# Two-stage attention on one core: every engine's order laid out by a plan inside the kernel, and stage 1 unfolded from an SBUF copy

## The chip, the cores and the metric

One core of a Trainium2 chip runs the whole kernel. The core has five engines with a queue each: TensorE (PE: matmuls, and PEld for the loading of its stationary operand), VectorE (DVE), ScalarE (ACT), GpSimd (POOL), and SyncE (SP), which here only issues DMAs. Each engine works off its own queue strictly in order; engines wait for each other by semaphores. The metric is the device time of one execution in microseconds (us), the median of several runs.

## The reference, cut to what matters

```python
# stage 1: attention in a window of 64, batch 8, 8 heads, 576 positions, head size 64
scores = q @ k.T / 8;  mask = (rel >= 0) & (rel < 64)
attn = softmax(where(mask, scores, -1e9))
x = (attn @ v).transpose(0, 2, 1, 3).reshape(8, 576, 512)
# stage 2: four experts e with causal attention of head size 64 over x, gated by the best two
logits = x @ w_gate;  w = softmax of the two largest logits, 0 for the others
q, k, v = x @ wq[e], x @ wk[e], x @ wv[e]
a = softmax(where(causal, q @ k.T / 8, -1e9))
out += w[e] * (a @ v @ wo[e])
```

All is float32. `wq` and `wk` are scaled by 8, so that the logits of stage 2 spread widely.

## The kernel before, in words

**Stage 1** works on blocks of 64 queries and two heads. Eight such blocks make a *unit* `u`, and there are 36 units; nine units make two batches. A unit has three steps:

- `s1_qk(u)`: 16 small matmuls into two PSUM banks `s1_u_0`, `s1_u_1` (tag `s`, five banks in all). ACT (L146) and DVE (L150) gather them into the SBUF tile `sm1_u`. Then comes the softmax: DVE takes the largest (L152), POOL subtracts (L153), ACT exponentiates (L154), DVE sums and inverts (L155 to L157), and POOL multiplies (L158).
- `s1_t(u)`: four transposes of `sm1_u` on PE into one PSUM bank `t1_u` (tag `t`, three banks in all; L168). The bank is unfolded into the SBUF tile `pt1_u`: for each half `e`, ACT copies 64 partitions (L172) and DVE multiplies the same 64 partitions by a mask (L173); afterwards POOL masks both ACT copies at once (L176).
- `s1_av(u)`: 16 small matmuls of `pt1_u` with V into the bank `o1_u` (tag `t`; L187), which ACT and DVE turn into `xh` and `xl`, a high and a low part (L200, L201).

**Stage 2** needs `xh`, `xl` of a whole batch. `s2_v`, `s2_k`, `s2_q` project (`v2ps`, `kps`, `qps`, tag `s`, L269 to L271); `s2_mm` makes the scores of two experts (banks `s2_…`, tag `s`, L385); `s2_soft` reads them on DVE (L400), exponentiates on ACT (L404) and weights on POOL (L441); `s2_t` transposes on PE (L450, banks `t2_…`, tag `t`) and ACT copies into `pt2` (L457 to L490); `s2_av_mm` multiplies by V (`o2`, tag `t`, L509); `s2_o` makes the output (`ops`, tag `s`, L530, and a DMA).

**What sets the order.** Each step has a position in time, worked out from tables of numbers (`POS`, `BPOS`, `LEAD`, `LAG`). The steps are sorted by position and called. One unit of position is half a batch of stage 2. Tile's own scheduler then decides what each queue holds: before position 1.0 and after 15.5 it orders all engines; between the two PE keeps the order of the calls (`manual_schedule` for PE), and the scheduler orders ACT, DVE and POOL.

Of the kernel before, what the change touches and what calls it, by code (L numbers as in the profile page):

```python
# [8 lines left out]
F32 = mybir.dt.float32  # L9
F32R = mybir.dt.float32r  # L10
# [7 lines left out]
NP = NH // 2  # L18
# [16 lines left out]

@with_exitstack
def window_attention_moe_attention(ctx: ExitStack, tc: tile.TileContext, qT, kT, vW,
                                   wg, wq, wk, wv, wo, out):
    nc = tc.nc
# [20 lines left out]

    P2 = [const.tile([128, 1024 * (part + 1)], F32, name=f"p2_{part}") for part in range(2)]
# [21 lines left out]
    make_identity(nc, ident)  # L83
# [45 lines left out]
    def s1_qk(u):  # L129

        banks = [psum.tile([128, 4, 128], F32, tag="s", bufs=5, name=f"s1_{u}_{x}") for x in range(2)]
        for x, j, p, b in tiles(u):
            c0 = 64 * int(b == 0)
            for h in range(2):
                r, o = slice(64 * h, 64 * h + 64), 64 * (h ^ x)
                nc.tensor.matmul(banks[x][o:o + 64, j, c0:], lhsT=pairs[p][0][r, 64 * b:64 * b + 64],  # L136
                                 rhs=pairs[p][1][r, 64 * b + c0:64 * b + 128], start=True, stop=True)
# [25 lines left out]
    def s1_t(u):  # L163

        ps = psum.tile([128, 4, 128], F32, tag="t", bufs=3, name=f"t1_{u}")
        sm = SM.pop(u).rearrange("r x j c -> r (x j c)")
        for i in range(4):
            nc.tensor.transpose(ps[:, i], sm[:, 128 * i:128 * i + 128], ident)  # L168
        t = PT1[u] = work.tile([128, 4, 2, 128], F32, tag="pt1", bufs=2, name=f"pt1_{u}")
        for e in range(2):  # L170
            r = slice(64 * e, 64 * e + 64)
            nc.scalar.activation(t[64:128, :, e], ps[r], AF.Copy)  # L172
            nc.vector.tensor_mul(t[0:64, :, e], ps[r],  # L173
                                 tri[r].rearrange("r a c -> r (a c)")[:, None, :].to_broadcast([64, 4, 128]))
        own_half = t[64:128].rearrange("r i e (a c) -> r (i e a) c", a=2)
        nc.gpsimd.affine_select(out=own_half, in_=own_half, pattern=[[0, 16], [1, 64]], base=0,  # L176
                                channel_multiplier=-1, compare_op=OP.is_ge, fill=0.0)
# [3 lines left out]
    def s1_av(u):  # L181
        t = PT1.pop(u)
        o = psum.tile([128, 8, 64], F32, tag="t", bufs=3, name=f"o1_{u}")
        for i, (x, j, p, b) in enumerate(tiles(u)):
            for h in range(2):
                c = 64 * (h ^ x)
                nc.tensor.matmul(o[64 * h:64 * h + 64, i], lhsT=pairs[p][2][:, h, b],  # L187
                                 rhs=t[:, 2 * x + j // 2, j % 2, c:c + 64], start=True, stop=True)
            if b == BLK - 1:
                freed.append(p)  # L190
# [82 lines left out]
    def s2_v(b, j):  # L273


        ps = psum.tile([128, 512], F32, tag="s", bufs=5, name=f"v2ps_{b}_{j}")
        for c in range(NP):
            if j < 4:
                xh, xl = (y[b][:, S * c + 128 * j:S * c + 128 * j + 128] for y in (XH, XL))
            else:  # L280
                xh, xl = (XT[b, x][:, c].rearrange("r a c -> r (a c)") for x in range(2))
            three(ps[:, :260], xh, xl, whi["v"][:, c], wlo["v"][:, c], c == 0, c == 3)
        src = ps[:, :256].rearrange("r (p s c) -> r p s c", p=2, s=2)
        dst = [V2[(b + i) % 2].rearrange("r j (p s) c -> r j p s c", s=2) for i in range(2)]
        if j < 4:
            nc.scalar.activation(dst[0][:, j, :, 0], src[:, :, 0], AF.Copy)
            vo = work.tile([128, 2, D], F32, tag="vo", bufs=2, name=f"vo_{b}_{j}")
            nc.scalar.activation(vo, src[:, :, 1], AF.Copy)
            for x in range(2):
                nc.gpsimd.tensor_scalar(dst[0][64 - 64 * x:128 - 64 * x, j, :, 1], vo[64 * x:64 * x + 64],  # L290
                                        1.0, 1.0, op0=OP.mult, op1=OP.mult)
        else:
            for i in range(2):
                for s in range(2):
                    nc.scalar.activation(dst[i][64 * s:64 * s + 64, 4, :, s], src[64 * i:64 * i + 64, :, s], AF.Copy)
        nc.vector.tensor_copy(L[b % 2][:, j], ps[:, 256:260])

    def s2_gate(b, j0, j1):
# [6 lines left out]
        tc.keep_in_program_order(nc.vector.tensor_tensor(g4[:, 0], lf, le, op=OP.is_gt))  # L305
# [27 lines left out]
    def proj(b, name, pr, half):  # L333
# [40 lines left out]
    def s2_mm(b, pr, k):  # L374
        banks = SB[b, pr, k] = [psum.tile([128, 512], F32, tag="s", bufs=5, name=f"s2_{b}_{pr}_{k}_{e}")
                                for e in range(2)]
        for i, key, n in SCORES[k]:
            q = slice(128 * i - 128, 128 * i)
            for x, (w, m) in enumerate(((0, 0), (0, 1), (1, 0))):
                for e in range(2):  # L380
                    r = slice(64 * e, 64 * e + 64)
                    rhs = KT[b, pr][r, m, key:key + n]
                    if e:
                        rhs = rhs.rearrange("r (a c) -> r a c", c=64)[:, ::-1]
                    nc.tensor.matmul(banks[e][:, at(i, e):at(i, e) + n], lhsT=QT[pr][r, w, q], rhs=rhs,  # L385
                                     start=x == 0, stop=x == 2)

# [55 lines left out]
    def s2_t(b, pr, part, k):  # L443
# [15 lines left out]
        if part == 0 and k == 0:  # L459
            for e in range(2):  # L460
                for i in (1, 2):
                    one(256 * e + 128 * i - 128, i, e, 0)
            nc.scalar.activation(pt[:, :, 64:320], ps.rearrange("r (e c) -> r e c", e=2), AF.Copy)
        elif part == 0 and k == 1:
            for e in range(2):
                one(128 * e, 2, e, 1)
            one(256, 1, 0, 1)
            one(384, 2, 0, 2)
# [6 lines left out]
        elif k < 2:  # L475
            for c in range(2):
                for i in (3, 4):
                    one(256 * c + 128 * i - 384, i, k, c)
            nc.scalar.activation(pt[:, k, 0:512], ps, AF.Copy)  # L479
        elif k == 2:  # L480
            for e in range(2):
                for i in (3, 4):
                    one(256 * e + 128 * i - 384, i, e, 2)
            nc.scalar.activation(pt[:, :, 512:768], ps.rearrange("r (e c) -> r e c", e=2), AF.Copy)
        else:
            for e in range(2):
                one(128 * e, 4, e, 3)
            one(256, 3, 0, 3)
            one(384, 4, 0, 4)
# [13 lines left out]
    def s2_av_mm(b, pr, part):  # L503
# [3 lines left out]
        for a, (c, x, w, q0) in enumerate(AVS[part]):  # L507
            for h in range(2):
                nc.tensor.matmul(o[64 * h:64 * h + 64, q0:q0 + w], lhsT=V2[b % 2][:, c, 2 * pr + h],  # L509
                                 rhs=PT2[part][:, h, x:x + w], start=a == 0, stop=a == len(AVS[part]) - 1,  # L510
                                 skip_group_check=True)

# [157 lines left out]
```

## Time and profile before

| | |
|---|---|
| median of 3 runs | 580.79 us (579.72 to 580.87) |
| profiled execution, its own time | 579.19 us |
| its span, from the first to the last instruction | 577.5 us |
| mean granted TensorE clock | 0.949 |
| PE busy / DVE / ACT / POOL | 482.2 / 358.8 / 321.9 / 230.5 us |
| instructions | 14663 |

The profiled execution took 1.7 us more than its span, and the median lies 1.6 us above the profiled execution. A window row gives, for a stretch of the span, its length, then the busy time of each engine with the number of instructions, and the granted clock. A row of the timeline gives start, duration, engine, line, operation and tiles (buffer numbers left out), and in brackets the idle time just before it with what ended it. A row of the waits gives who waited for whom: total, number of times, and the longest.

### The profile page before, as it was taken

To read this page: it belongs to the slowest core of one execution; us is meant where nothing else is said; L and a number is where in the kernel's file an instruction comes from. 1 tells how busy PE (TensorE), PEld (TensorE's weight loads), DVE (VectorE), ACT (ScalarE), POOL (GpSimd) and SP (SyncE) were. 2 spreads that over 40 slices of the span, in tenths; PEclk is the share of its full clock that TensorE was granted. 3 is DMA by queue.
4 is the path that set the end of the run, shared out by engine and by line. 5 is a ranking of instruction groups with operands and counts; after the bars stand their busy time and mean duration, and the time that the engine had idled before them with its cause. 6 is when DMAs were issued, how large, how long until landed. Compare 5 with 4: busy or idle time off the path is not lost. (4 is left out here: it accounts for less than half of the span.)

```text
span 577.5 us, 14663 instructions
## 1 busy us (share of the span) xinstructions
PE 482.2 (84%) x5672; PEld 430.0 (74%) x5672; DVE 358.8 (62%) x1178; ACT 321.9 (56%) x965; POOL 230.5 (40%) x403
## 2 busy tenths in 40 slices
PE   4488859599697987959789895996969889999996
PEld 3377758588586967858688794985858888899874
DVE  5977857558366774746656675574746567556452
ACT  3555455647357573655547565473555756565671
POOL 5656343532445342253333534244334442241330
PEclk9999978989799997979989899898989989999999
DMA  8574411122252222221333220231224100010112
GB/s 308 221 223 150 134 42 45 44 86 77 82 188 72 83 78 84 60 75 52 104 144 123 85 86 37 86 100 51 77 80 147 58 2 22 19 56 2 38 38 92
DMA packets 20630, 51.29 MB, mean 89 GB/s; under 512 B 2768, under 2 KB 3280, under 8 KB 20560
## 3 DMA queue, kind: packets, MB, share of 16 engines
q1 hardware_dynamic: 20560, 50.35, 26.4%
q8 instruction: 45, 0.74, 0.5%
q14 instruction: 25, 0.20, 0.1%
HBM read 40.90 MB, written 9.44 MB: 87 GB/s over the span
## 5 line engine op out<-in xcount | busy, mean ns | idle before, releaser
L404 ACT ACTIVATE p<-p,r 128x192 f32<-128x192 f32 (+3 forms) x128 | 77.3, 605 | 50.6 <-DVE r L424 29.5
L441 POOL TENSOR_SCALAR p<-p,r 128x192 f32<-128x192 f32 (+3 forms) x128 | 72.7, 586 | 65.8 <-DVE r L437 44.0
L173 DVE TENSOR_TENSOR pt<-t,tri 64x512 f32<-64x512 f32 x72 | 49.4, 687 | 38.5 <-ACT pt L172 36.8
L168 PE MATMUL t<-ident,sm 128*128 128x128 f32 x144 | 27.8, 325 | 48.8 <-POOL sm L158 48.6
L187 PE MATMUL o<-pt,v 128*64 128x64 f32 x1152 | 49.0, 250 | 22.1 <-POOL pt L176 22.1
L400 DVE CUSTOM_DVE_ANT_0 p<-s,causal 128x320 f32<-128x320 f32 (+3 forms) x160 | 66.5, 472 | 0.7
L187 PEld LDWEIGHTS o<-pt,v 128*64 128x64 f32 x1152 | 44.0, 162 | 29.6 <-POOL pt L176 25.3
L172 ACT ACTIVATE pt<-t 64x512 f32<-64x512 f32 x72 | 42.5, 591 | 39.6 <-PE t L168 26.8
L450 PE MATMUL t<-ident,p 128*128 128x128 f32 x384 | 52.5, 276 | 11.7 <-ACT pt L479 11.4
L176 POOL TENSOR_SCALAR_AFFINE_SELECT pt<-pt 64x1024 f32<-64x1024 f32 x36 | 41.6, 1155 | 51.2 <-ACT pt L172 21.4
L154 ACT ACTIVATE sm<-sm 128x512 f32<-128x512 f32 x36 | 22.7, 631 | 67.1 <-POOL sm L153 67.1
L155 DVE TENSOR_REDUCE st<-sm 128x8 f32<-128x512 f32 x36 | 24.7, 685 | 56.5 <-ACT sm L154 56.4
L168 PEld LDWEIGHTS t<-ident,sm 128*128 128x128 f32 x144 | 18.9, 164 | 54.4 <-POOL sm L158 53.5
L158 POOL TENSOR_TENSOR sm<-sm,st 128x512 f32<-128x512 f32 x36 | 38.3, 1065 | 52.8 <-DVE st L157 32.2
L153 POOL TENSOR_TENSOR sm<-sm,st 128x512 f32<-128x512 f32 x36 | 38.5, 1070 | 49.3 <-DVE st L152 39.8
L450 PEld LDWEIGHTS t<-ident,p 128*128 128x128 f32 x384 | 42.9, 141 | 17.0 <-ACT pt L479 13.5
L509 PE MATMUL o<-pt,v 128*64 128x128 f32 (+3 forms) x896 | 55.4, 280 | 0.0
L136 PE MATMUL s<-k,q 64*64 64x128 f32 (+1 forms) x1152 | 49.1, 301 | 6.3 <-DMA k<-in_kT_dram 6.3
L509 PEld LDWEIGHTS o<-pt,v 128*64 128x64 f32 x896 | 51.0, 152 | 1.6 <-ACT pt L457 0.4
L136 PEld LDWEIGHTS s<-k,q 64*64 64x64 f32 x1152 | 38.1, 152 | 14.9 <-DMA q<-in_qT_dram 7.0
L385 PE MATMUL s<-kt,qt 64*128 64x256 f32 (+2 forms) x480 | 45.1, 323 | 0.3 <-DVE qt L359 0.2
L269 PE MATMUL kps<-xh,wkhi 128*128 128x320 f32 (+1 forms) x128 | 41.5, 324 | 0.0
(127 smaller groups left out, 1263.6 us busy)
## 6 DMA issues: line engine op xcount, KB each, us to landing
v<-in_vW_dram SPq DMA_DIRECT2D x32, 576.0 KB, 4.0
k<-in_kT_dram SPq DMA_DIRECT2D x32, 320.0 KB, 4.0
q<-in_qT_dram SPq DMA_DIRECT2D x32, 288.0 KB, 3.1
out_dram<-out SPq DMA_DIRECT2D x32, 256.0 KB, 2.0
out_dram<-out SPq DMA_DIRECT2D x8, 128.0 KB, 2.3
pt<-in_wv_dram SPq DMA_DIRECT2D x1, 512.0 KB, 8.8
pt<-in_wk_dram SPq DMA_DIRECT2D x1, 512.0 KB, 7.9
pt<-in_wq_dram SPq DMA_DIRECT2D x1, 512.0 KB, 8.7
```

The source lines that it names most:

```text
L136: nc.tensor.matmul(banks[x][o:o + 64, j, c0:], lhsT=pairs[p][0][r, 64 * b:64 * b + 64], rhs=pairs[p][1][r, 64 * b + c0:64 * b + 128], star ...
L168: nc.tensor.transpose(ps[:, i], sm[:, 128 * i:128 * i + 128], ident)
L172: nc.scalar.activation(t[64:128, :, e], ps[r], AF.Copy)
L173: nc.vector.tensor_mul(t[0:64, :, e], ps[r], tri[r].rearrange("r a c -> r (a c)")[:, None, :].to_broadcast([64, 4, 128]))
L176: nc.gpsimd.affine_select(out=own_half, in_=own_half, pattern=[[0, 16], [1, 64]], base=0, channel_multiplier=-1, compare_op=OP.is_ge, fill ...
L187: nc.tensor.matmul(o[64 * h:64 * h + 64, i], lhsT=pairs[p][2][:, h, b], rhs=t[:, 2 * x + j // 2, j % 2, c:c + 64], start=True, stop=True)
L385: nc.tensor.matmul(banks[e][:, at(i, e):at(i, e) + n], lhsT=QT[pr][r, w, q], rhs=rhs, start=x == 0, stop=x == 2)
L400: nc.vector.tensor_tensor_reduce(out=dst, in0=ps, in1=mask, scale=1.0, scalar=3.0e38, op0=OP.add, op1=OP.min, accum_out=to)
L404: nc.scalar.activation(p, p, AF.Exp, bias=r2[:, 0, x:x + 1], scale=-1.0, accum_out=r2[:, 1, x:x + 1])
L441: nc.gpsimd.tensor_scalar(p, p, r2[:, 3, x:x + 1], 1.0, op0=OP.mult, op1=OP.mult)
L450: nc.tensor.transpose(ps[:, col:col + 128], P2S[pr][part][:, at:at + 128], ident)
L509: nc.tensor.matmul(o[64 * h:64 * h + 64, q0:q0 + w], lhsT=V2[b % 2][:, c, 2 * pr + h], rhs=PT2[part][:, h, x:x + w], start=a == 0, stop=a ...
```

## The change

Three things are changed. No position in the tables is.

1. Calls to the engines are recorded by a class `Plan` and not issued at once. A call becomes an entry with its engine, its tiles, its position (`at`) and a length in ns from formulas for each engine. Matmuls inside `nc.block()` are one entry that isn't broken up.
2. `Plan.link` finds which entries must follow which, from the regions that they read and write. `Plan.order` then walks through time with a clock for each engine: whenever an engine is free, it takes, of the entries whose inputs are done by the lengths and whose buffers are free, the one with the earliest position. The entries are issued in the order in which they were taken, and `manual_schedule` for all engines keeps that order.
3. `s1_t` copies the whole bank `t1_u` to an SBUF tile `ft_u` with one ACT instruction. DVE multiplies from `ft_u`, and POOL masks from `ft_u` into `pt1_u`, one half each, so that there are two POOL instructions of half the size.

Since all instructions come out of one loop, every instruction carries the line of that loop in the changed program (L227).

```diff
+class Plan:
+    OVERLAP = {"V": 85, "A": 105, "G": 30, "P": 0, "S": 0}
+    SWITCH = 105
+    HOP = 40
...
+    def length(self, engine, name, outs, ins):
+        n = outs[0].free_size()
+        psum = any(x.space == PSUM for x in ins)
+        if engine == "A":
+            return (165 if psum else 205) + 0.83 * n + (230 if len(outs) > 1 else 0)
+        if engine == "V":
+            n = max([n] + [x.free_size() for x in ins])
+            return 152 + 1.04 * n + (65 if len(outs) > 1 else 0)
+        if engine == "G":
+            return {"tensor_tensor": 60 + 1.97 * n, "affine_select": 190 + 0.94 * n,
+                    "memset": 100 + 0.8 * n}.get(name, 265 + 0.85 * n)
+        if engine == "S":
+            return outs[0].nbytes() / 290 + 60
...
+    def order(self):
...
+            for e in "PAVGS":
+                if clock[e] > now:
+                    continue
+                short, best = set(), None
+                for op in sorted(queues[e], key=lambda o: (self.place(o, mode), o["n"])):
+                    need = {}
+                    for t in op.get("takes", ()):
+                        need[t["tag"]] = need.get(t["tag"], 0) + 1
+                    lack = {k for k, v in need.items() if k in short or free[k] < v}
+                    if lack:
+                        short |= lack
+                        continue
+                    if op["ready"] <= now:
+                        best = op
+                        break
...
+                best["start"] = now
+                clock[e] = now + max(20, cost - self.OVERLAP[e])
+                end = now + cost + {"P": 200, "S": 2000}.get(e, 0)
...
+    def issue(self):
+        for op in self.order():
+            for call, args, kw in op["calls"]:
+                call(*args, **kw)
...
 def s1_t(u):
...
+        f = work.tile([128, 4, 128], F32, tag="ft", bufs=2, name=f"ft_{u}")
+        nc.scalar.activation(f, ps, AF.Copy)
         for e in range(2):
             r = slice(64 * e, 64 * e + 64)
-            nc.scalar.activation(t[64:128, :, e], ps[r], AF.Copy)
-            nc.vector.tensor_mul(t[0:64, :, e], ps[r],
+            nc.vector.tensor_mul(t[0:64, :, e], f[r],
                                  tri[r].rearrange("r a c -> r (a c)")[:, None, :].to_broadcast([64, 4, 128]))
-        own_half = t[64:128].rearrange("r i e (a c) -> r (i e a) c", a=2)
-        nc.gpsimd.affine_select(out=own_half, in_=own_half, pattern=[[0, 16], [1, 64]], base=0,
-                                channel_multiplier=-1, compare_op=OP.is_ge, fill=0.0)
+            nc.gpsimd.affine_select(out=t[64:128, :, e].rearrange("r i (a c) -> r i a c", a=2),
+                                    in_=f[r].rearrange("r i (a c) -> r i a c", a=2), pattern=[[0, 4], [0, 2], [1, 64]],
+                                    base=0, channel_multiplier=-1, compare_op=OP.is_ge, fill=0.0)
...
-    for t0, t1, fixed in ((-99, FIXED[0], False), (FIXED[0], FIXED[1], True), (FIXED[1], 99, False)):
-        with tc.manual_schedule(engines={mybir.EngineType.PE}) if fixed else nullcontext():
-            for t, f, args in todo:
-                if t0 <= t < t1:
-                    f(*args)
+    for t, f, args in todo:
+        nc.at = t
+        f(*args)
+    with tc.manual_schedule():
+        nc.issue()
```

What this moves in the queues is shown at unit 20, in the middle of the program. `sm1_20` is its softmax, `t1_20` its transposes, and `o1_19` the result of unit 19. First PE before, from the last matmuls of `s1_qk(20)` to the transposes of `s1_t(20)` (repeating rows of `v2ps` left out):

```order
L136 MATMUL s1_20_0_3203<-k18_2606,q18_2604 64x128 x2
L450 MATMUL t2_2_0_1_0_3240<-ident_90,p2_1_68 128x128 x4
L450 MATMUL t2_2_0_1_1_3246<-ident_90,p2_1_68 128x128 x4
L269 MATMUL v2ps_3_2_3252<-wvhi_436,xh3_2018 128x260
...
L450 MATMUL t2_2_0_1_2_3271<-ident_90,p2_1_68 128x128 x4
L450 MATMUL t2_2_0_1_3_3277<-ident_90,p2_1_68 128x128 x4
L269 MATMUL v2ps_3_3_3285<-wvhi_436,xh3_2018 128x260
...
L168 MATMUL t1_20_3304<-ident_90,sm1_20_3221 128x128 x4
L187 MATMUL o1_19_3315<-pt1_19_3178,v16_2424 64x64 x2
```

And PE now, between the same two places (repeating rows of `v2ps`, `s2`, `s1_21` and `kps` left out):

```order
L227 MATMUL t2_2_0_1_0_534<-ident_82,p2_1_68 128x128 x4
L227 MATMUL v2ps_3_2_536<-wvhi_151,xh3_369 128x260
...
L227 MATMUL s2_2_1_2_0_548<-kt_2_1_454,qt1_88 128x320
...
L227 MATMUL s1_21_0_552<-k18_449,q18_448 64x128 x2
...
L227 MATMUL t2_2_0_1_3_539<-ident_82,p2_1_68 128x128 x4
L227 MATMUL o1_19_545<-pt1_19_524,v17_456 64x64 x14
L227 MATMUL v2ps_3_3_540<-wvhi_151,xh3_369 128x260
...
L227 MATMUL kps_3_0_0_558<-xh3_369,wkhi_168 128x320
...
L227 MATMUL o2_2_0_1_547<-pt2_1_84,v2_0_97 64x128 x12
L227 MATMUL t1_20_542<-ident_82,sm1_20_530 128x128 x4
```

Between `s1_qk(20)` and `t1_20` stood 16 transposes and the 24 matmuls of two `v2ps`; now the scores `s2_2_1_2` and `s2_2_1_3` (12 matmuls), the 16 matmuls of `s1_21`, the 16 of `o1_19`, the 12 of one `kps` and the 18 of `o2_2_0_1` stand there as well.

On POOL before, from the subtraction of unit 20 to the mask of its unfolded tile:

```order
L176 AFFINE_SELECT pt1_19_3178<-pt1_19_3178 64x1024
L290 TENSOR_SCALAR v2_1_119<-vo_3_1_3198 64x2x64 x2
L148 MEMSET sm1_21_3403 128x64
L153 TENSOR_TENSOR sm1_20_3221<-sm1_20_3221,st1_20_3222 128x512
L290 TENSOR_SCALAR v2_1_119<-vo_3_2_3266 64x2x64 x2
L158 TENSOR_TENSOR sm1_20_3221<-sm1_20_3221,st1_20_3222 128x512
L290 TENSOR_SCALAR v2_1_119<-vo_3_3_3299 64x2x64 x2
L176 AFFINE_SELECT pt1_20_3309<-pt1_20_3309 64x1024
```

And on POOL now:

```order
L227 AFFINE_SELECT pt1_19_524<-ft_19_525 64x4x128
L227 TENSOR_SCALAR v2_1_98<-vo_3_1_527 64x2x64 x2
L227 TENSOR_TENSOR sm1_20_530<-sm1_20_530,st1_20_531 128x512
L227 TENSOR_SCALAR v2_1_98<-vo_3_2_537 64x2x64 x2
L227 MEMSET sm1_21_554 128x64
L227 TENSOR_SCALAR p2_2_69<-p2_2_69,r2_2_1_521 128x576 x2
L227 TENSOR_SCALAR v2_1_98<-vo_3_3_541 64x2x64
L227 TENSOR_TENSOR sm1_20_530<-sm1_20_530,st1_20_531 128x512
L227 TENSOR_SCALAR v2_1_98<-vo_3_3_541 64x2x64
L227 TENSOR_TENSOR sm1_21_554<-sm1_21_554,st1_21_555 128x512
L227 AFFINE_SELECT pt1_20_543<-ft_20_544 64x4x128 x2
```

Two weightings `p2_2` of stage 2 now stand between the two POOL steps of unit 20's softmax, and the subtraction of unit 21 goes ahead of the masks of unit 20, which are two. On DVE the multiplications of unit 20 now read `ft_20`, with the end of unit 21's softmax between them:

```order
L227 TENSOR_REDUCE st1_21_555<-sm1_21_554 128x8
L227 TENSOR_TENSOR pt1_20_543<-ft_20_544,tri_81 64x4x128
L227 TENSOR_SCALAR st1_21_555<-st1_21_555 128x8
L227 COPY g2_1_96<-gt_3_0_565 64x4x2x2
L227 TENSOR_TENSOR pt1_20_543<-ft_20_544,tri_81 64x4x128
L227 RECIPROCAL st1_21_555<-st1_21_555 128x8
```

Before, `xl4`, which needs the result of unit 19, stood between the two multiplications of unit 20; now the end of unit 21's softmax and a copy of the gates do.

More of the change, by code (lines that the diff above doesn't have):

```diff
@@ L1 @@
-from contextlib import ExitStack, nullcontext
+import heapq
+from contextlib import ExitStack, contextmanager
 import concourse.bass as bass
@@ L6 @@
 from concourse._compat import with_exitstack
-from concourse.masks import make_identity
 F32 = mybir.dt.float32
@@ L36, in window_attention_moe_attention, with __init__, __getattr__, later @@
+class Queue:
+    def __init__(self, plan, engine, letter):
+        self.plan, self.engine, self.letter = plan, engine, letter
+    def __getattr__(self, name):
+        call = getattr(self.engine, name)
+        def later(*args, **kw):
+            self.plan.add(self.letter, call, name, args[0] if args else kw["out"], args, kw)
+        return later
 @with_exitstack
@@ L131, in s1_qk @@
         banks = [psum.tile([128, 4, 128], F32, tag="s", bufs=5, name=f"s1_{u}_{x}") for x in range(2)]
[L132 to L137, printed above, removed]
+        with nc.block():
+            for x, j, p, b in tiles(u):
+                c0 = 64 * int(b == 0)
+                for h in range(2):
+                    r, o = slice(64 * h, 64 * h + 64), 64 * (h ^ x)
+                    nc.tensor.matmul(banks[x][o:o + 64, j, c0:], lhsT=pairs[p][0][r, 64 * b:64 * b + 64],
+                                     rhs=pairs[p][1][r, 64 * b + c0:64 * b + 128], start=True, stop=True)
         sm = SM[u] = work.tile([128, 2, 4, 64], F32, tag="sm1", bufs=3, name=f"sm1_{u}")
@@ L183, in s1_av @@
         o = psum.tile([128, 8, 64], F32, tag="t", bufs=3, name=f"o1_{u}")
[L184 to L190, printed above, removed]
+        with nc.block():
+            for i, (x, j, p, b) in enumerate(tiles(u)):
+                for h in range(2):
+                    c = 64 * (h ^ x)
+                    nc.tensor.matmul(o[64 * h:64 * h + 64, i], lhsT=pairs[p][2][:, h, b],
+                                     rhs=t[:, 2 * x + j // 2, j % 2, c:c + 64], start=True, stop=True)
+                if b == BLK - 1:
+                    freed.append(p)
         i = 0
@@ L376, in s2_mm @@
                                 for e in range(2)]
[L377 to L386, printed above, removed]
+        with nc.block():
+            for i, key, n in SCORES[k]:
+                q = slice(128 * i - 128, 128 * i)
+                for x, (w, m) in enumerate(((0, 0), (0, 1), (1, 0))):
+                    for e in range(2):
+                        r = slice(64 * e, 64 * e + 64)
+                        rhs = KT[b, pr][r, m, key:key + n]
+                        if e:
+                            rhs = rhs.rearrange("r (a c) -> r a c", c=64)[:, ::-1]
+                        nc.tensor.matmul(banks[e][:, at(i, e):at(i, e) + n], lhsT=QT[pr][r, w, q], rhs=rhs,
+                                         start=x == 0, stop=x == 2)
     def s2_mm0(b, pr):
@@ L506, in s2_av_mm @@
         o = OB[b, pr, part] = psum.tile([128, 512], F32, tag="t", bufs=3, name=f"o2_{b}_{pr}_{part}")
[L507 to L511, printed above, removed]
+        with nc.block():
+            for a, (c, x, w, q0) in enumerate(AVS[part]):
+                for h in range(2):
+                    nc.tensor.matmul(o[64 * h:64 * h + 64, q0:q0 + w], lhsT=V2[b % 2][:, c, 2 * pr + h],
+                                     rhs=PT2[part][:, h, x:x + w], start=a == 0, stop=a == len(AVS[part]) - 1,
+                                     skip_group_check=True)
     def s2_av_out(b, pr, part):
```

222 lines of the change are left out of this document (187 added, 35 removed).

## The prediction

> **What bounds the kernel now.** I read the page first, then the waits of PE, then stretches of the span, then the timeline around one long wait. The shares of busy time:
>
> ```profile
> PE 482.2 (84%) x5672; PEld 430.0 (74%) x5672; DVE 358.8 (62%) x1178; ACT 321.9 (56%) x965; POOL 230.5 (40%) x403
> ```
>
> PE leads by far, so its idle time is what an order can win. The waits of PE name it:
>
> ```profile
> PE t L168 <- POOL sm L158: 48.6, 16, 5.0
> PE o L187 <- POOL pt L176: 22.1, 12, 5.1
> PE t L450 <- ACT pt L479: 11.4, 9, 1.5
> PE s L136 <- DMA k<-in_kT_dram: 6.3, 3, 4.4
> ```
>
> The first two belong to stage 1: PE stands at the transposes of a unit whose softmax isn't done, or at the matmuls of a unit whose tile isn't unfolded. The stretches show where the idle time lies: the start up to unit 9, the long middle where both stages run, and the end, with its last matmuls.
>
> ```profile
> core 0: us, PE busy (x) PEld busy (x) DVE busy (x) ACT busy (x) POOL busy (x), PEclk, DMA share, GB/s
> 0.00:74.50 74.50, 52.47 (x720) 44.74 (x720) 56.41 (x133) 37.88 (x90) 40.19 (x85) 1.00 0.60 201
> ...
> 74.50:506.30 431.80, 364.98 (x4344) 328.35 (x4344) 268.02 (x905) 243.44 (x742) 171.97 (x281) 0.93 0.24 77
> 506.30:570.60 64.30, 63.16 (x606) 55.94 (x605) 32.90 (x139) 40.56 (x134) 18.31 (x37) 1.00 0.10 36
> ```
>
> In the middle PE idles 431.80 - 364.98 = 66.8 us. In the end, where no stage 1 softmax is waited for, it idles 1.1 of 64.3. The granted clock in the middle is 0.93, in the end 1.00. Asked for exactly the twelve stretches of the middle that were granted 0.50 (first, last and their sum):
>
> ```profile
> 78.36:85.18 6.82, 4.41 (x43) 4.30 (x44) 2.48 (x5) 1.23 (x2) 4.13 (x6) 0.50 0.19 45
> ...
> 464.06:467.47 3.41, 3.41 (x54) 3.41 (x54) 2.71 (x6) 1.33 (x3) 1.47 (x3) 0.50 0.02 5
> sum 58.03, PE 47.16 PEld 44.17 DVE 24.34 ACT 18.79 POOL 19.25; mean PE 3.93 PEld 3.68 DVE 2.03 ACT 1.57 POOL 1.60
> ```
>
> PE is busy for 47.16 us at half the clock, so 23.6 us of its busy time would go at the full clock. These stretches follow waits of PE. One of them in full, unit 20 (the row at 243.56 is its `s1_qk`):
>
> ```profile
> 243.56 1.10 PE L136 MATMUL s<-k,q 64*64 64x128 f32 x32
> ...
> 246.47 0.77 DVE L150 COPY_PREDICATED sm<-own,s 128x256 f32<-128x256 uint8 x2
> ...
> 247.31 0.69 DVE L173 TENSOR_TENSOR pt<-t,tri 64x512 f32<-64x512 f32 x1
> ...
> 248.03 0.69 DVE L152 TENSOR_REDUCE st<-sm 128x8 f32<-128x512 f32 x1
> ...
> 249.29 1.14 POOL L176 TENSOR_SCALAR_AFFINE_SELECT pt<-pt 64x1024 f32<-64x1024 f32 x1
> ...
> 250.50 0.67 POOL L290 TENSOR_SCALAR v<-vo 64x128 f32<-64x128 f32 x2
> ...
> 251.35 1.04 POOL L153 TENSOR_TENSOR sm<-sm,st 128x512 f32<-128x512 f32 x1
> ...
> 252.42 0.63 ACT L154 ACTIVATE sm<-sm 128x512 f32<-128x512 f32 x1 [3.70 <-POOL sm L153]
> ...
> 254.39 1.04 POOL L158 TENSOR_TENSOR sm<-sm,st 128x512 f32<-128x512 f32 x1 [1.26 <-ACT pt L457]
> ...
> 255.49 1.11 PE L168 MATMUL t<-ident,sm 128*128 128x128 f32 x4 [4.99 <-POOL sm L158]
> ...
> 256.53 1.98 PE L187 MATMUL o<-pt,v 128*64 128x64 f32 x32
> ```
>
> From the end of `s1_qk(20)`, at 244.66, to its transposes pass 10.8 us, and PE stands idle for the last 4.99 of them, while unit 20's steps wait behind the mask of unit 19 and copies of `v2` on POOL. The matmuls behind the wait take 1.98 us, where the same 32 records take 1.11 elsewhere (a row further down).
>
> **The plan's order on PE.** The order lists in the section on the change show what PE has in hand between `s1_qk(20)` and `t1_20`. I price the added pieces with these rows:
>
> ```profile
> 445.64 1.03 PE s L136 x30
> ...
> 448.38 1.11 PE o L187 x32
> ...
> 495.56 1.76 PE o L509 x36
> ...
> 497.32 1.00 PE s L385 x12
> ...
> 73.71 0.31 PE L270 MATMUL qps<-xl,wqhi 128*128 128x320 f32 x1
> 73.86 0.31 PE L271 MATMUL qps<-xh,wqlo 128*128 128x320 f32 x1
> ```
>
> The x counts two records for each matmul of `s1`, `o1` and `o2`. The added pieces are the scores of two key blocks (1.0), `s1_21` (1.0), `o1_19` (1.1), one `kps` of twelve matmuls that start 0.15 apart (1.8) and `o2` of 18 (1.8): 6.7 us. With the 4.7 us that stood there before (16 transposes and 24 matmuls of `v2ps`), PE now has 11.4 us in hand, against the 10.8 of the softmax. So the 4.99 go if the softmax is no slower than before. I counted the same for all units of the middle, by the order lists and such rows. Before, the work between `s1_qk` and the transposes swings from 1.4 to 13.4 us by unit, in a pattern that repeats every nine; now it lies between 7.1 and 14.2, and in all nine places of the pattern it is at least as long as the softmax took in the trace (6.1 to 10.8). I take the softmax waits of the middle as gone. What comes next are `o1` and the `o2`.
>
> **The unfolding.** Its groups, and the same steps for unit 20:
>
> ```profile
> L173 DVE TENSOR_TENSOR pt<-t,tri 64x512 f32<-64x512 f32 x72 | 49.4, 687 | 38.5 <-ACT pt L172 36.8
> ...
> L172 ACT ACTIVATE pt<-t 64x512 f32<-64x512 f32 x72 | 42.5, 591 | 39.6 <-PE t L168 26.8 <-DVE pt L173 11.7
> ...
> L176 POOL TENSOR_SCALAR_AFFINE_SELECT pt<-pt 64x1024 f32<-64x1024 f32 x36 | 41.6, 1155 | 51.2 <-ACT pt L172 21.4 <-issue 21.0 <-PE s L136 5.7
> ...
> 256.64 0.59 ACT L172 ACTIVATE pt<-t 64x512 f32<-64x512 f32 x1 [1.93 <-PE t L168]
> ...
> 259.84 1.14 POOL L176 TENSOR_SCALAR_AFFINE_SELECT pt<-pt 64x1024 f32<-64x1024 f32 x1 [3.67 <-ACT pt L172]
> ...
> 3.64 0.72 POOL L87 TENSOR_SCALAR_AFFINE_SELECT tri<-tri 64x128 f32<-64x128 f32 x2
> ```
>
> ACT: 36 copies fewer, 36 x 0.59 = 21 us of busy time, none of it on PE's path by itself. POOL: a mask of 128 columns takes 0.36 us and one of 1024 takes 1.14, so one of 512 is estimated at 0.36 + 384 x 0.78/896 = 0.69; two of them are 1.39 for 1.14, 9 us more in all; POOL has room (172 of 431.8). DVE: the trace has no multiplication of this form from SBUF; the sum over 512 columns of an SBUF tile takes what this one takes from PSUM (0.69 both), so I keep 0.69. The chain for one unit was copy, multiplication, copy, mask, at least 0.59 + 0.69 + 0.59 + 1.14 = 3.0 us, 4.3 for unit 20. Now it is 0.59 and then 1.39, DVE and POOL side by side: 2.0. The bank `t1_u` is free after 0.59 instead of after the second multiplication, which takes from the 11.4 us of waits for banks (t L450).
>
> **A cost that the plan's lengths don't have.** DVE now reads two SBUF tiles while POOL reads SBUF too. Rows of that kind:
>
> ```profile
> 15.88 1.57 DVE L114 SCALAR_TENSOR_TENSOR wvlo<-pt,wvhi 128x1040 fp32r<-128x1040 f32 x1
> ...
> 16.31 2.04 POOL L153 TENSOR_TENSOR sm<-sm,st 128x512 f32<-128x512 f32 x1
> ...
> 254.94 0.57 DVE L306 TENSOR_TENSOR g<-logits 128x64 f32<-128x64 f32 x1
> ...
> L306 DVE TENSOR_TENSOR g<-logits 128x16 f32<-128x16 f32 x4 | 0.7, 166 | 0.0
> ```
>
> POOL's subtraction took 2.04 us instead of 1.04 while DVE worked on two SBUF tiles, and DVE's comparison of 64 columns ran until POOL's multiplication of 254.39 was done. So the two multiplications and the two masks of a unit may run one after another: 2 x 0.69 + 2 x 0.69, 1.4 us later than side by side. Bounds for the 27 units of the middle: 0 and 27 x 1.4 = 37 us at PE. PE has between 4.2 and 15.5 us of work between `t1` and `o1` by the new order, against 0.59 + 2.8 = 3.4 of an undisturbed chain, but the engines are shared: before, 12 of 36 units made PE wait for the mask. I take half the upper bound, 18 us, and 2 us for `o2`, where the work in hand falls from between 2.6 and 6.5 us to between 1.1 and 4.3.
>
> The Trainium skill (SBUF — State Buffer, Who interferes with whom) says that a DVE instruction with two SBUF inputs and a GpSimd instruction that reads SBUF exclude each other, the later one blocking fully. The rows above agree; by this rule alone the term would be its upper end, 37 us instead of 18.
>
> **The sum.** Middle: 431.8 - 66.8 - 23.6 = 341.4 us with no wait and the full clock. To it come 20 us of waits and 4 us for one or two stretches of half clock that still follow a wait (47.16 / 12 / 2 = 2.0 each): 365.4, so 66.4 less. The start I leave as it is: its waits are one unit's softmax after the other with nothing else to do, and the loads come in the same order; its bounds, from its 22.0 us of idle time in the first stretch, are a fifth less and a quarter more: -4 and +6. The end is PE without waits, bounds -3 and +3. SP issues the same DMAs; PE waited for them only in the first 13 us. Recording and issuing cost nothing on the chip: there are 36 copies fewer on ACT and 36 masks more on POOL. Span 577.5 - 66.4 = 511.1, with 1.7 outside it 512.8, and the median 1.6 above the profiled execution: **514 us**. A change of 0.2% (1.2 us) is about what a measurement can tell here.
>
> **The rivals.**
>
> - *The ports decide.* POOL and DVE block each other in every unit and for other work too (a weighting of POOL is 0.59 on average, half of it more per unit): 27 x 1.7 = 46 us of waits, and half of the half clock stays, 12 us. Middle 341.4 + 46 + 12 = 399, 32 less: **548**. For it: the rows of contention. Against: the work in hand. This is also the skill's rule at its full price.
> - *The order only moves the waits.* The lengths don't hold, PE meets as many late inputs as before, and 66.8 and 23.6 stay; the unfolding's 21 us of ACT are off the path: **580**. For it: every queue is now fixed, so one late step delays all behind it, and the lengths know neither the port nor the half clock. Against: the counts of work in hand.
> - *Slower: the fixed order of DVE.* DVE's queue can no longer take what is ready; a multiplication that waits for POOL holds the score reads (L400) behind it, and their banks hold PE. DVE is busy 268 of 431.8 us; squeezed into 365 that is 73%, and 54 multiplications that each wait for a POOL step of 1.04 make it 89%. It decides from 90.4 / 27 = 3.3 us of PE wait and slow clock per unit; at 4.5 us the middle is 463 and the time **612**. Against it: DVE still idles 11% then, and ACT and POOL more.
> - *No wait is left:* 580.8 - 90.4 = **490**; this is the floor.
>
> **The numbers.** My forecast with its floor 0.68, the ports 0.19, moved waits 0.06 (half of it within 0.2%), slower 0.07. From 492 to 546 lie most of the forecast and of the ports' case, 0.8 together. Faster 0.90, same 0.03, slower 0.07.
>
> **What will show it.** Right: PE's wait at `t1` for `sm1` falls from 48.6 to under 15; granted clock above 0.98; PE busy above 91% of the span. The port: multiplications from `ft` with a mean above 0.69 and masks above 0.7 us. Wrong: new PE waits for banks that DVE or ACT hold, or a middle still at 0.93 of the clock.

## The result, and the profile after

The changed kernel took **515.12 us** (median, 512.70 to 516.96), the kernel before 580.83 us on the same chip: a ratio of 0.887 (95%: 0.883 to 0.891), 65.7 us less. The profiled execution of the changed kernel took 516.96 us, the longest one timed, and its span is 515.2. All rows of the changed program carry the line of the issuing loop, L227, so groups are told apart by engine and tiles.

The shares of busy time on the page of the kernel after:

```profile
PE 476.6 (93%) x5672; PEld 417.5 (81%) x5672; DVE 371.2 (72%) x1178; ACT 299.0 (58%) x929; POOL 262.7 (51%) x439
```

PE was 84% busy before. What PE waited for, in the whole span of the kernel after (us in total, times, longest):

```profile
PE t L227 <- POOL sm L227: 10.2, 10, 3.1
PE s L227 <- DMA k<-in_kT_dram: 7.9, 4, 4.7
PE o L227 <- DVE pt L227: 3.9, 3, 2.6
PE o L227 <- POOL pt L227: 3.6, 4, 1.8
```

The transposes' wait for the softmax fell from 48.6 to 10.2, the wait of `o1` for POOL's mask from 22.1 to 3.6 (with 3.9 more for DVE's half of the same tile, all of it in the start), and the 11.4 of `t2` for free banks have left the head of the list. In the middle alone (first the kernel before, from 74.5 to 506.3 us; then after, from 76 to 438.1) the softmax waits are nearly gone:

```profile
PE t L168 <- POOL sm L158: 44.1, 12, 5.0
PE t L450 <- ACT pt L479: 11.4, 9, 1.5
PE o L187 <- POOL pt L176: 11.2, 5, 5.1
```

```profile
PE t L227 <- POOL sm L227: 3.5, 5, 0.8
PE o L227 <- POOL pt L227: 1.4, 2, 0.7
```

The same three stretches as before (start up to `s1_9`, middle up to the first `v2ps` of the last batch, end), columns as in the prediction; the last row is the only stretch of the middle that was granted half the clock:

```profile
0.00:76.00 76.00, 53.57 (x722) 46.58 (x722) 58.91 (x133) 31.95 (x80) 46.05 (x92) 0.89 0.58 197
76.00:438.10 362.10, 352.89 (x4338) 310.74 (x4337) 276.82 (x899) 225.65 (x716) 198.33 (x310) 1.00 0.29 91
438.10:508.90 70.80, 68.55 (x612) 59.23 (x611) 34.09 (x145) 41.38 (x134) 18.34 (x37) 0.95 0.10 35
...
81.79:85.20 3.41, 3.41 (x39) 2.75 (x40) 1.26 (x8) 1.08 (x3) 2.84 (x5) 0.50 0.21 34
```

The middle is 69.7 us shorter (431.8 to 362.1): 57.6 of it is idle time of PE (66.8 to 9.2). Its half clock went from 58 us to 3.4. The start is 1.5 longer, the end 6.5.

Unit 20 again, in the timeline of the kernel after (the rows are of `s1_qk(20)`, its softmax, and `t1_20`):

```profile
216.60 1.10 PE L227 MATMUL s<-k,q 64*64 64x128 f32 x32
...
220.05 0.69 DVE L227 TENSOR_REDUCE st<-sm 128x8 f32<-128x512 f32 x1
...
224.32 1.04 POOL L227 TENSOR_TENSOR sm<-sm,st 128x512 f32<-128x512 f32 x1
...
228.24 1.09 POOL L227 TENSOR_TENSOR sm<-sm,st 128x512 f32<-128x512 f32 x1
...
229.88 0.66 PE L227 MATMUL t<-ident,sm 128*128 128x128 f32 x4
```

From the end of `s1_qk(20)` at 217.70 the softmax takes until 229.33: 11.6 us, more than the 10.8 of before. The row of `t1_20` has no bracket: PE didn't wait, since it had work until 229.88. The softmax wasn't made faster; it was covered.

### The profile page after: what moved, and what is told of

Its sections match the earlier page's. It is cut to its first block, busy times and chain, and to the rows that moved or that the text cites. A ratio compares the mean times of both kernels' runs of the same rounds, so it can differ in the third digit from the quotient of the medians.

```text
span 515.2 us, 14666 instructions
## 1 busy us (share of the span) xinstructions
PE 476.6 (93%) x5672; PEld 417.5 (81%) x5672; DVE 371.2 (72%) x1178; ACT 299.0 (58%) x929; POOL 262.7 (51%) x439
## 4 chain that ended last, share of the span: by engine, by line
PE 66%; DVE 13%; POOL 12%; ACT 3%; issue 3%; DMA 1%; SPq 0%; POOLq 0%; DVEq 0%
PE s L227 14%; PE o L227 12%; PE t L227 11%; PE ops L227 10%; PE v2ps L227 8%; PE qps L227 7%; PE kps L227 5%; POOL p L227 5%; DVE st L227 4%; POOL sm L227 4%; POOL pt L227 3%; DVE g L227 2%; DVE p L227 1%; DMA k<-in_kT_dram 1%; DVE sm L227 1%
## 5 line engine op out<-in xcount | busy, mean ns | idle before, releaser
L227 POOL TENSOR_TENSOR sm<-sm,st 128x512 f32<-128x512 f32 x72 | 77.6, 1078 | 72.3 <-DVE st L227 52.7
L227 PE MATMUL o<-pt,v 128*64 128x64 f32 (+3 forms) x2048 | 95.3, 250 | 9.1 <-DVE pt L227 3.9
L227 PEld LDWEIGHTS o<-pt,v 128*64 128x64 f32 x2048 | 85.6, 144 | 20.1 <-POOL pt L227 9.5
L227 ACT ACTIVATE p<-p,r 128x192 f32<-128x192 f32 (+3 forms) x128 | 77.4, 607 | 31.9 <-DVE r L227 31.5
L227 POOL TENSOR_SCALAR_AFFINE_SELECT pt<-ft 64x512 f32<-64x512 f32 x72 | 64.4, 894 | 61.5 <-ACT ft L227 58.3
L227 POOL TENSOR_SCALAR p<-p,r 128x192 f32<-128x192 f32 (+3 forms) x128 | 77.9, 625 | 31.9 <-DVE r L227 14.8
L227 ACT ACTIVATE pt<-t 128x512 f32<-128x512 f32 (+2 forms) x192 | 69.5, 388 | 22.1 <-PE t L227 20.1
L227 DVE CUSTOM_DVE_ANT_0 p<-s,causal 128x320 f32<-128x320 f32 (+3 forms) x160 | 68.2, 470 | 7.1 <-PE s L227 6.6
L227 DVE TENSOR_TENSOR pt<-ft,tri 64x512 f32<-64x512 f32 x72 | 62.6, 869 | 4.8 <-ACT ft L227 3.5
L227 DVE TENSOR_REDUCE st<-sm 128x8 f32<-128x512 f32 x72 | 49.1, 684 | 17.0 <-ACT sm L227 15.8
L227 PE MATMUL t<-ident,p 128*128 128x128 f32 x384 | 59.2, 283 | 1.6 <-POOL p L227 1.5
L227 PE MATMUL s<-kt,qt 64*128 64x256 f32 (+2 forms) x480 | 55.0, 334 | 2.7 <-DVE sm L227 1.1
L227 PE MATMUL s<-k,q 64*64 64x128 f32 (+1 forms) x1152 | 45.5, 298 | 7.9 <-DMA k<-in_kT_dram 7.9
L227 PEld LDWEIGHTS t<-ident,p 128*128 128x128 f32 x384 | 44.3, 144 | 10.4 <-issue 2.7
L227 PEld LDWEIGHTS s<-k,q 64*64 64x64 f32 x1152 | 36.5, 151 | 14.7 <-issue 6.1
L227 DVE COPY_PREDICATED sm<-own,s 128x256 f32<-128x256 uint8 x72 | 30.5, 444 | 24.4 <-POOL sm L227 13.3
L227 PEld LDWEIGHTS s<-kt,qt 64*128 64x128 f32 x480 | 36.2, 185 | 13.0 <-issue 3.8
L227 PE MATMUL qps<-xh,wqhi 128*128 128x320 f32 (+1 forms) x128 | 40.7, 318 | 0.0
L227 PE MATMUL kps<-xh,wkhi 128*128 128x320 f32 (+1 forms) x128 | 39.6, 310 | 0.0
L227 ACT ACTIVATE sm<-sm 128x512 f32<-128x512 f32 x36 | 22.7, 630 | 28.2 <-POOL sm L227 27.8
L227 PE MATMUL v2ps<-wvhi,xh 128*128 128x260 f32 x128 | 38.8, 303 | 0.0
L227 PE MATMUL qps<-xl,wqhi 128*128 128x320 f32 (+1 forms) x128 | 37.8, 295 | 0.0
```

Source lines behind the costliest of these rows:

```text
L227: call(*args, **kw)
```

## The experiments

### Which part of the change is it?

**The plan with the old unfolding.** `s1_t` as before the change (two ACT copies, multiplication from PSUM, one mask of 1024), everything else as after.

```diff
-        f = work.tile([128, 4, 128], F32, tag="ft", bufs=2, name=f"ft_{u}")
-        nc.scalar.activation(f, ps, AF.Copy)
...
+            nc.scalar.activation(t[64:128, :, e], ps[r], AF.Copy)
```

> The plan alone, with the unfolding of before (two ACT copies, two DVE multiplications from PSUM, one POOL mask). Theory A (PE's order is what pays: it has work in hand while a unit's softmax runs, so the waits and the half clock behind them go): 515 to 525 us, PE's wait for the softmax still under 15 us, ACT 21 us busier. Rival B (the unfolding pays, by a shorter chain, 21 us less of ACT and a bank that is free earlier): 540 us or more.

Measured: 508.55 us (508.02 to 509.37), ratio 0.878 (0.875 to 0.880), below the range of theory A, whose two signs came: PE's wait for the softmax is 8.5 us, and ACT is 28 us busier (327.0). The plan alone brings 71 us (579.69 before, on the same chip); the new unfolding, put on top of it, costs 6.6 us by the medians, 5.4 by the ratios.

**The new unfolding without the plan.** The kernel before with the `s1_t` of after.

> The unfolding from the SBUF copy alone, in the kernel before, with Tile's scheduler as it was. Theory A: 570 to 585 us, the waits of PE for the softmax stay near 48 us and the clock near 0.95. Rival B: 550 us or less.

Measured: 594.75 us (593.87 to 595.68), ratio 1.026 (1.023 to 1.029): slower by 15 us than before on the same chip, above both ranges. The groups of the unfolding in this run:

```profile
L174 DVE TENSOR_TENSOR pt<-ft,tri 64x512 f32<-64x512 f32 x72 | 64.9, 901 | 27.2 <-ACT ft L171 26.4
...
L176 POOL TENSOR_SCALAR_AFFINE_SELECT pt<-ft 64x512 f32<-64x512 f32 x72 | 63.2, 878 | 70.8 <-ACT ft L171 57.0 <-DVE r L438 10.9
```

The multiplication takes 901 ns on average where it took 687 from PSUM. With either order the new unfolding is a loss, although ACT has 36 copies fewer.

**The plan orders PE's queue only.** All is recorded and planned as after, but Tile's scheduler orders the other queues.

```diff
-    with tc.manual_schedule():
+    with tc.manual_schedule(engines={mybir.EngineType.PE}):
```

> The plan fixes PE's queue alone; Tile's scheduler orders ACT, DVE, POOL and SP again, by its own costs. Theory A in its strong form (PE's order is enough): 513 to 525 us. Rival D (the order of the other engines is as much of the gain, since a softmax step that stands behind other work makes PE wait whatever PE's order is): 535 us or more, with PE's waits for sm and pt back above 30 us.

Measured: 548.66 us (548.04 to 550.75), ratio 0.947 (0.944 to 0.950). PE's waits:

```profile
PE t L227 <- POOL sm L227: 14.7, 5, 4.1
PE o L227 <- POOL pt L227: 9.8, 13, 2.1
PE s L227 <- DMA k<-in_kT_dram: 8.5, 4, 4.5
PE s L227 <- DVE logits L227: 8.3, 5, 2.9
```

All of the 14.7 us lie in the first 77 us; behind them PE doesn't wait for a softmax once. But many shorter waits come up that after hardly has: banks that DVE still reads (`logits`, 8.3 for 1.0) and masks (9.8 for 3.6). PE's order alone is not enough; the time is that of rival D, though its waits for `sm` and `pt` come to 24.5 and not to above 30.

**The plan orders all queues but PE's.** PE keeps the order of the calls between positions 1.0 and 15.5, as before, and the plan orders ACT, DVE, POOL and SP around it. The plan of this run also lets a PSUM bank be started before the tile `xh` or `xl` that it will be read into is free.

```diff
-                        if not u["bank"] and u["first"]["n"] > first["n"]:
+                        if not u["bank"] and u["tag"][:2] not in ("xh", "xl") and u["first"]["n"] > first["n"]:
...
+        calls = sorted((o for o in ops if o["engine"] == "P"), key=lambda o: (o["at"], o["n"]))
...
+                    if e == "P" and op is not calls[0] and (FIXED[0] <= op["at"] < FIXED[1] or op["at"] >= FIXED[1] > calls[0]["at"]):
+                        continue
...
```

> The plan orders ACT, DVE, POOL and SP, but PE keeps the order of the calls between positions 1.0 and 15.5, as in the kernel before (unfolding from the SBUF copy). With the run where PE's queue alone was planned (548.7 us) this completes a two by two. Theory A (work in hand on PE is what counts): 560 to 575 us, waits of about 4 us at the units with 1.4, 4.7 and 4.9 us of work in hand stay. Rival D (the order of the other engines is the larger half, by shorter softmax chains): 530 us or less.

Measured: 583.40 us (582.08 to 584.61), ratio 1.007 (1.005 to 1.010). PE's first wait in this run:

```profile
PE t L232 <- POOL sm L232: 57.7, 21, 7.4
```

Of the 57.7 us, 49.9 lie between 75 and 510 us. With PE's order as before, the waits stay, by Tile's order of the other queues (57.2 in the run with the new unfolding alone) and by the plan's. None of the ranges expected held this: the other queues bring less than I gave them. With the new unfolding in all four, the parts of the order make a square:

| | other queues by Tile | other queues by the plan |
|---|---|---|
| PE in call order | 594.75 | 583.40 |
| PE by the plan | 548.66 | 515.12 |

PE's order alone brings 46.1 us, the other queues alone 11.4, both 79.6. The remaining 22 us come only when both are laid out by one plan.

**Flat lengths.** The plan counts 500 ns for every instruction of ACT, DVE and POOL.

```diff
+        if engine in "AVG":
+            return 500
```

> The changed kernel, but the plan takes every ACT, DVE and POOL instruction to last 500 ns (PE and the loads keep their lengths). Theory M (the measured lengths make the order good, since work in hand must match the true length of a softmax): 525 to 550 us, with PE's waits for sm and pt back to 20 us or more. Rival G (any order that goes by readiness over all queues together does it, and a rough length is enough): 512 to 520 us.

Measured: 531.30 us (529.94 to 533.05), ratio 0.918 (0.915 to 0.920), in the range of theory M; PE waits 15.2 us for `sm` and 6.5 for POOL's `pt`. 16.2 of the 65.7 us hang on the lengths of these three engines; the other 49.5 come with lengths that say only that every step takes a while.

### What does the new unfolding cost, and how?

**The multiplication reads PSUM.** As after, but DVE multiplies from the bank `t1_u`; ACT still copies to `ft_u` for POOL. All queues hold the same instructions in the same order as after, so only what DVE reads differs.

```diff
-            nc.vector.tensor_mul(t[0:64, :, e], f[r],
+            nc.vector.tensor_mul(t[0:64, :, e], ps[r],
```

> The changed kernel, only that DVE multiplies from the PSUM bank and not from the SBUF copy; every queue keeps its order. It has one SBUF input then, so that POOL and DVE need not exclude each other. Multiplications should fall from 869 to about 690 ns and masks from 894 to about 670 ns in both theories. Theory A (the work in hand on PE covers the port): 512 to 517 us, within 0.5% of the changed kernel. Rival C (the port costs PE about what its waits for pt show, 9 us with the PEld waits): 503 to 508 us.

Measured: 504.59 us (504.10 to 504.91), ratio 0.871 (0.868 to 0.873), 10.5 us below the changed kernel (9.4 by the ratios; the changed kernel's own runs scatter most, by 4 us). The groups, first after, then this run:

```profile
L227 POOL TENSOR_SCALAR_AFFINE_SELECT pt<-ft 64x512 f32<-64x512 f32 x72 | 64.4, 894 | 61.5 <-ACT ft L227 58.3
...
L227 DVE TENSOR_TENSOR pt<-ft,tri 64x512 f32<-64x512 f32 x72 | 62.6, 869 | 4.8 <-ACT ft L227 3.5
```

```profile
L227 DVE TENSOR_TENSOR pt<-t,tri 64x512 f32<-64x512 f32 x72 | 49.4, 686 | 5.5 <-ACT ft L227 4.3
L227 POOL TENSOR_SCALAR_AFFINE_SELECT pt<-ft 64x512 f32<-64x512 f32 x72 | 49.1, 681 | 64.2 <-ACT ft L227 61.0
```

POOL's mask wasn't touched, and yet it falls from 894 to 681 ns. One place in both timelines, after first, then this run:

```profile
202.00 0.66 POOL L227 TENSOR_SCALAR_AFFINE_SELECT pt<-ft 64x512 f32<-64x512 f32 x1 [1.61 <-ACT ft L227]
202.05 2.60 DVE L227 TENSOR_TENSOR pt<-ft,tri 64x512 f32<-64x512 f32 x2
202.75 1.35 POOL L227 TENSOR_TENSOR sm<-sm,st 128x512 f32<-128x512 f32 x1
```

```profile
194.63 0.66 POOL L227 TENSOR_SCALAR_AFFINE_SELECT pt<-ft 64x512 f32<-64x512 f32 x1 [1.63 <-ACT ft L227]
194.81 1.38 DVE L227 TENSOR_TENSOR pt<-t,tri 64x512 f32<-64x512 f32 x2
195.37 1.04 POOL L227 TENSOR_TENSOR sm<-sm,st 128x512 f32<-128x512 f32 x1
```

The two multiplications take 2.60 us instead of 1.38, and POOL's subtraction, next to them, 1.35 instead of 1.04. DVE and POOL slow each other here; this is the contention that the prediction calls the port. The expectation that the work in hand hides it fell. The time is in the range of rival C, but by another way than C gives: PE's waits for `pt` fall only from 7.5 to 4.9 us. The middle of this run:

```profile
72.00:426.40 354.40, 350.72 (x4339) 309.72 (x4337) 269.14 (x899) 227.88 (x716) 177.31 (x310) 1.00 0.29 93
```

It is 7.7 us shorter than that of after, 5.5 of it idle time of PE and 2.2 busy time. Of the 12.6 us between the spans of the two profiled executions, 4.0 lie in the start and 0.9 in the end.

**The same without the plan.** The kernel before, with the copy to `ft_u` for POOL and the multiplication from PSUM.

> The kernel before with Tile's scheduler and the unfolding from the SBUF copy for POOL, but DVE multiplies from PSUM. With the SBUF copy for both it took 594.8 us. Theory P (that loss is DVE and POOL excluding each other): 575 to 583 us, multiplications at 690 ns. Rival S (the loss is another order that Tile's scheduler made, with two POOL masks and later softmax steps): 588 to 597 us.

Measured: 577.31 us (575.91 to 578.79), ratio 0.997 (0.995 to 0.998). Against 594.75 with the multiplication from `ft_u`, the run that reads PSUM is 17 us shorter under Tile's scheduler. Mask and multiplication take 684 and 687 ns here. The scheduler's queues in the two runs are nearly but not quite the same (25 of 1178 DVE instructions and 128 of 5672 matmul records are out of the common order), so a part of the 17 us can lie in the order. The single copy by itself is then a small gain, 0.3% here; under the plan it is 4.0 us, from 508.55 with the old unfolding to 504.59.

**The right lengths.** As after, but the plan counts 869 ns for the multiplication of 512 columns from `ft` and 894 for the mask of 512, as measured.

```diff
+            if name == "tensor_mul" and n == 512 and not psum:
+                return 869
...
+            if name == "affine_select" and n == 512:
+                return 894
```

> The changed kernel (515.1 us) with two lengths of its plan raised to what the trace showed: 869 ns for a multiplication of 512 columns from ft, 894 ns for a mask of 512 columns. Theory M (the plan's order was wrong because its lengths leave the exclusion of VectorE and GpSimd out, and the lost time is a matter of order): with the lengths put right most of the 10.5 us that reading from PSUM saved comes back, 505 to 510 us. Rival L (the exclusion costs engine time on VectorE and GpSimd itself, which no order gives back): 512 to 518 us, with multiplications and masks still near 0.87 and 0.89 us on average.

Measured: 509.05 us (507.61 to 510.03), ratio 0.879 (0.876 to 0.881): inside the range of the first theory. 6.1 of the 10.5 us come back, while the instructions still take this long (861 and 886 ns on average).

**The same order without the contention.** The queues of the run before, the multiplication from PSUM.

> The plan's order of the previous run (869 and 894 ns for the multiplication and the mask, 509.05 us), with the same queues, but the multiplication reads PSUM, so that the exclusion is gone, as in the run of 504.59 us with the changed kernel's order. With the changed kernel and these two runs it makes a square: order by the old or by the raised lengths, with or without the exclusion. Theory M (raised lengths only make the order fit the exclusion): without the exclusion they bring nothing, 503.5 to 507 us. Rival O (the order by the raised lengths happens to be better by itself, 6 us with or without the exclusion): 496.5 to 500.5 us.

Measured: 502.88 us (502.65 to 504.14), ratio 0.869 (0.867 to 0.871), just below the range of the first theory.

| | multiplication from `ft` | from PSUM |
|---|---|---|
| the change's lengths | 515.12 | 504.59 |
| 869 and 894 ns | 509.05 | 502.88 |

The new order is worth 6.1 us with the contention and 1.7 without (4.8 and 1.2 by the ratios). So most of what it brings is that it fits the contention, as theory M has it. That the order is also better by itself isn't shown: the 1.7 us lie within the intervals of the two ratios (0.868 to 0.873, and 0.867 to 0.871). The contention then still costs 6.2 us that no order tried here gave back.

### The end

**Output blocks split in two.** As the run that multiplies from PSUM, but in the last batch each output block is two blocks of three matmuls, so that a half of one can fill a gap of PE, as Tile's scheduler did before the change.

```diff
-        with nc.block():
-            for pr in range(2):
...
+        for prs in (((0,), (1,)) if b == NB - 1 else ((0, 1),)):
+            with nc.block():
+                for pr in prs:
...
```

> The kernel that multiplies from PSUM (504.6 us), and in the last batch the two halves of each output block may be taken apart by the plan, so that PE has them in hand while the last softmax runs. Theory E (the end got slower because unbroken blocks left PE nothing to fill with, 2.6 us of waits and 1.7 of half clock): 501 to 503 us. Rival: the end is set by the chain of the last softmax, 504 to 506 us.

Measured: 502.85 us (502.55 to 503.33), ratio 0.868 (0.867 to 0.870), inside the range of theory E, 1.7 us less than without the split (1.3 by the ratios) and level with the 502.88 above. The waits at this place, in the timeline of after, of the run that multiplies from PSUM, and of this run:

```profile
490.53 0.33 PE L227 MATMUL t<-ident,px 128*128 128x128 f32 x1 [1.65 <-POOL px L227]
490.70 0.60 PE L227 MATMUL t<-ident,p 128*128 128x128 f32 x4
491.83 1.41 PE L227 MATMUL t<-ident,p 128*128 128x128 f32 x4 [0.54 <-POOL p L227]
```

```profile
478.83 0.33 PE L227 MATMUL t<-ident,px 128*128 128x128 f32 x1 [1.64 <-POOL px L227]
```

```profile
479.07 0.33 PE L227 MATMUL t<-ident,px 128*128 128x128 f32 x1 [0.19 <-POOL px L227]
```

The four transposes at 491.83 take 1.41 us where those at 490.70 take 0.60: the clock had halved in between, at 491.39.

## Why the prediction was right, and where it was not

Predicted 514, measured 515.1. The mechanism held, but terms were off in both directions; that they add up to within 1.1 us is luck.

- **The softmax waits of the middle go: right.** 44.1 us became 3.5 in all, with a softmax that is no faster at unit 20. That PE's order is what does it is shown by two runs: planned alone it leaves none of these waits after the first 77 us; left as before it leaves 49.9 us of them between 75 and 510 us.
- **The floor of 341.4 us for the middle: about 10 too low.** After, PE is busy for 352.89 us there; less half of the 3.41 us at half clock, 351.2. The number of matmuls hardly differs (4338 records for 4344). Their order does. The step that failed is taking PE's busy time in the old order as the floor of the new one: the new order has a price of its own, which the sum put at nothing. A matmul whose stationary operand has another size than the one before it (the numbers with a star in a row, as 64*128 after 128*128) starts 0.22 us after it on average in the trace before and 0.21 in the one after. Counted over the records of the middle, there are 119 such changes before and 187 after: the score matmuls stood 12 or 18 in a row before and stand mostly six in a row after, between other work. Against the mean start of the same kind of matmul without a change, one costs 0.12 us by the trace after and 0.14 by the one before. 68 changes more are then an estimated 8 to 10 us of the 10. No run varies this alone, so it is counted and not tested. A smaller part is the way I read idle time:

```profile
161.74 0.38 PE L227 MATMUL s<-kt,qt 64*128 64x256 f32 x1
162.46 0.60 PE L227 MATMUL s<-kt,qt 64*128 64x256 f32 x5 [0.34 <-DVE logits L227]
```

  In the second row matmuls start some 0.1 us apart, so the pause between the two rows costs about 0.6 us. The wait counts 0.34 of it, since a matmul counts as busy until its modelled end. In the score blocks of the middle after, six pauses of this kind cost 4.4 us by the starts, of which 2.7 count as idle, so 1.7 us of busy time are pauses; before there is none.
- **Waits of 20 us: mis-sized, 9.2 measured.** Its main part was the 18 us at `o1`, half of the port's upper bound. In the middle `o1` waits for the mask 1.4 us in all, and without the contention the middle is 7.7 us shorter. The port's price came by another road: longer instructions on DVE (72 x 0.183 = 13.2 us against the run from PSUM) and POOL (72 x 0.213 = 15.3 us) in all units; POOL as a whole is 25.8 us less busy without it (262.7 to 236.9). In the time all this is 10.5 us. My two durations of 0.69 us, which left the contention to the term of waits, were right only without it: 0.686 and 0.681 against 0.869 and 0.894. The lengths of the plan have the same fault.

  The Trainium skill (SBUF — State Buffer, Who interferes with whom) has the exclusion that these rows show, and the traces agree. Its full price of 37 us on PE's path wasn't paid: the pair didn't meet everywhere (half of the multiplications took 720 ns or less, by the row below), and where it did, work in hand took a part.

```profile
L227 DVE TENSOR_TENSOR pt<-ft,tri x72: 672/720/1424, 16.0 to 424.6; 64x512 f32<-64x512 f32 x72
```

  Its columns are the shortest, the median and the longest in ns.
- **Half clock of 4 us: 1.7.** One stretch of 3.41 us in the middle.
- **The sum of the middle.** 351.2 + 9.2 + 1.7 = 362.1 against 341.4 + 20 + 4 = 365.4. The floor and the waits were off by 10 each, in opposite directions.
- **The end, -3 to +3: wrong, +6.5.** I took it as PE without waits. After, its idle time is 2.2 us instead of 1.1, and the 6.34 us busy at half clock cost 3.2; the rest, 2.2 of busy time, I can't place but for six more records. The step that failed is "the end unchanged": unbroken output blocks can't fill a wait that was filled before. The split took the half clock and 1.4 us of idle time away. The start, +1.5, lay inside its bounds.
- **ACT's 21 us are off the path: right.** ACT has 22.9 us less to do after (321.9 to 299.0); with the old unfolding it has 327.0 and the kernel is faster. POOL's increase was underestimated: 9 us expected, 32 measured, of which 15 are the contention in the masks.
- **Time outside the span and the median.** 1.7 us lie outside, as predicted; but the median lies 1.8 below the profiled execution, where it lay 1.6 above before. That term was only the scatter of one execution, and it closed the gap left by the span (515.2 measured, 511.1 predicted): luck.
- **The signs.** PE's wait for `sm1` under 15 us (10.2), PE busy above 91% (93%) and the port's two signs came. The granted clock didn't come in the profiled execution, with 0.974 and not 0.98; over the four executions it lies from 0.970 to 0.992, in two of them above 0.98. In the profiled one, start and end have the half clock (0.89 and 0.95), the middle hardly any.
- **The rivals.** "The ports decide" (548) had the right mechanism at some four times its price (46 us of waits, 10.5 measured in all). "The order only moves the waits" (580) and "the fixed order of DVE" (612) didn't come; DVE is 76% busy in the middle (276.82 of 362.10), close to the 73% that the slower case started from, but the 89% it needed didn't come.

## What to carry to other kernels

Read from the trace how long a chain takes after the work that starts it, and how much work PE holds in hand until it needs the result: where the second is at least as long as the first at every place, the wait goes even if the chain gets longer. Order all queues by one plan, since PE's order without the others gave 46 of 80 us, and the others without PE's 11. Count what the new order itself adds on the busiest engine, as here the changes between sizes of matmul. Before an operand is moved from PSUM to SBUF to relieve one engine, see which pair of engines will then read SBUF together; and give a planner the lengths under that contention, not those of an engine alone.

## What the runs showed of the hardware

**The half clock follows how busy PE was in a fixed window.** Each trace's clock rows lie on a grid of 3.41 us. The grid's window that holds the wait for `px` at the end, in the kernel after, and the corresponding one of the run with split output blocks:

```profile
487.97:491.39 3.42, 1.68 (x15) 1.07 (x12) 1.99 (x12) 3.35 (x11) 1.23 (x4) 1.00 0.00 0
```

```profile
479.31:482.73 3.42, 2.69 (x33) 1.96 (x33) 0.94 (x3) 3.24 (x11) 2.84 (x7) 1.00 0.01 2
```

With PE busy 1.68 us in the window, the next 6.82 us ran at half clock; with 2.69 the clock stayed. Over the twelve traces here, counted on that grid over pairs of neighbouring windows that lie inside the span: after 62 full-clock windows with PE busy below 1.5 us the next was at half clock every time; from 1.5 to 2.34 us, 10 times of 71, and what decides there is open; above it never in 1511. Back to full clock it went after none of the 45 half-clock windows with less than 2.74 us busy, after 6 of 16 up to 3.14, and after all 66 with more. Waits need not be long for this: the window of 1.68 us held one wait of 1.65. By these counts a planner need not remove each wait, only keep PE busy for some 2.4 of each 3.41 us; the middle after has one window that failed this, with 2.33 us busy from 78.37.

The Trainium skill (TensorE: Matmul & The Clock Gate, HAM oscillation — how this bites in real kernels) gives the rule as no idle gaps of more than about 3.4 us. The length agrees with the grid here, the gap does not: here one of 1.65 us was enough.

**A DVE instruction that reads two SBUF tiles slows POOL as well as itself**, on 64 partitions too: 869 and 894 ns on average for 686 and 681, in one place two multiplications in 2.60 us for 1.38.

**A matmul whose stationary operand has another size than the one before it starts later**: 0.22 and 0.21 us after it on average, over 109 such changes in the middle before and 185 after, all at full clock, where the four transposes of one `t` start 0.11 us apart.
